# Sorted attention and a bilinear feed-forward: the output product by one level of Strassen's seven products

## The chip, the cores and the metric

The kernel runs on one core of a Trainium2 chip. Its engines work in parallel, each through its own queue in order: TensorE (PE in the profile; PEld is its loading of weights, which overlaps the matmuls), VectorE (DVE), ScalarE (ACT), GpSimd (POOL) and SyncE (SP), which here only issues DMAs. GpSimd issues the loads, SyncE the stores and the DMA transposes. The metric is the device time of one execution in microseconds (us); less is better.

## What is computed

```python
# q, k, v: (4, 8, 768, 64) = batch, heads, tokens, head size; sort_net: (4, 8, 8, 8)
P = sort_net
for _ in range(5):                                   # Sinkhorn
    P = np.exp(P - np.max(P, axis=-1, keepdims=True))
    P = P / (np.sum(P, axis=-1, keepdims=True) + 1e-09)
    P = P / (np.sum(P, axis=-2, keepdims=True) + 1e-09)
# blocks of 96 tokens; k and v become mixtures of their 8 blocks
k_sorted = np.einsum('bhij,bhjcd->bhicd', P, k_b)
v_sorted = np.einsum('bhij,bhjcd->bhicd', P, v_b)
scores = scale * np.matmul(q_b, k_sb.transpose(0, 1, 2, 4, 3))   # inside each block
attn = softmax(scores)
x = np.matmul(attn, v_sb)                            # heads side by side: (3072, 512)
out = ((x @ w_a) * (x @ w_b)) @ w_out                # 512 -> 1536 -> 512, float32
```

## The kernel before

Everything is computed in bf16 with f32 accumulation. Work goes by batch (4) and, in the attention, by pair of heads (4 pairs a batch, `g` counts all 16).

*Attention of one pair.* `stage_mix` (L265) multiplies k, and then v, by the expanded sort matrix `s_all` (24 matmuls for the two) and evicts the result into `kT` and `vT`; a DMA transpose turns `vT` into `vs` (L283). `stage_q` (L260) is the DMA transpose of q, from a copy that GpSimd makes (`pair_q`, L254). `stage_scores` (L286) multiplies and takes the exponential into `eT`. `stage_o` (L301) multiplies `eT` by `vs` (L241, with a column of ones for the sums), DVE takes the reciprocal (L245) and multiplies (L247), and `to_xT` (L307) transposes the result by DMA into `xT`.

*Batch 0* is done in two halves of four blocks each, with transposes on PE instead of by DMA: `half_q` (L170), `half_mix`, `half_scores`, `half_v`, `half_o`, `half_x`. Its q is loaded in two halves of 64 rows (`load_q_half`, L81), the second after the first weights. The four `half_q` of the first half run before the Sinkhorn chain has ended, the four of the second between the matmuls of the feed-forward.

*Feed-forward.* `ffn_ab(b, m, t)` (L331) makes one of the 12 row tiles `m` of the hidden layer for half `t` of the batch's 768 tokens: four matmuls of 384 columns with `w_a`, four with `w_b` (L323), ACT casts the first result (L343), DVE multiplies (L344) into `hT`. `ffn_out(b, c)` (L347) makes 128 output rows: 12 matmuls of 512 columns (L351) accumulate in one bank, ACT or DVE copies it (L160, L162), SyncE stores it.

*Order.* PE, GpSimd and SyncE run in the order in which the program is written; DVE and ACT are ordered by a scheduler, but for the head of the kernel. `interleave` (L529) spreads the pieces of the next batch's attention ("units") over the steps of the feed-forward of this batch: 12 `ffn_ab` and 6 `ffn_out` in the second half of batch 0, 24 and 6 in a later batch. Units come as mix, output of the pair before, scores. The loads of pair `g + 4` are issued with the mix of pair `g`; GpSimd is not tied to PE's progress but by the buffers it needs, of which `ld` has 8 for each of k, v and q.

*PSUM.* `psA` has two buffers of two banks (mix, scores, output), `psF` four of one bank (feed-forward and the small transposes).

*Head.* Five Sinkhorn rounds alternate ACT and DVE; PE then waits with warm-up matmuls (`keep_busy`, L164) for the replicated matrix and brings it into columns (`to_columns`, L410), from which `s_all` is spread.

Of the kernel before, what the change touches and what calls it, by code (L numbers as in the profile page):

```python
# [22 lines left out]
def kernel(  # L23
# [11 lines left out]
    nc = tc.nc  # L35
# [11 lines left out]
    HP = H // 2  # L47
    KA = DMODEL // P
    KO = DFF // P
    NBH = NB // 2  # L50
# [6 lines left out]
    HW = S // 2  # L57
    PSUM = bass.MemoryType.PSUM
# [3 lines left out]
    ld = ctx.enter_context(tc.tile_pool(name="ld", bufs=8))  # L62
    qtp = ctx.enter_context(tc.tile_pool(name="qtp", bufs=5))
    xtp = ctx.enter_context(tc.tile_pool(name="xtp", bufs=2))
    att = ctx.enter_context(tc.tile_pool(name="att", bufs=4))
    ffp = ctx.enter_context(tc.tile_pool(name="ffp", bufs=2))
    psA = ctx.enter_context(tc.tile_pool(name="psA", bufs=2, space=PSUM))
    psF = ctx.enter_context(tc.tile_pool(name="psF", bufs=4, space=PSUM))

# [9 lines left out]
    q_first = const.tile([P, H, W], BF16, name="q_first")  # L79

    def load_q_half(h):  # L81
        nc.gpsimd.dma_start(out=q_first[h * PH:(h + 1) * PH],
                            in_=_ap(q, h * PH * W, [[W, PH], [S * D, H], [1, W]]))

    loaded = {}

    def load_pair(b, hp):
        tiles = []
        for name, t in (("k2", k), ("v2", v), ("q2", q)):
            base = (b * H + 2 * hp) * S * D  # L90
            if b == 0 and name == "q2":
                continue
            to = ld.tile([P, 2, W], BF16, tag=name, name=name)
            nc.gpsimd.dma_start(out=to, in_=_ap(t, base, [[W, P], [S * D, 2], [1, W]]))  # L94
            tiles.append(to)
        loaded[b * HP + hp] = tiles

# [3 lines left out]
    WC = 256  # L101
# [12 lines left out]
    load_q_half(0)  # L114
    make_identity(nc, ident, nomemset=True)
    for hp in range(HP):
        load_pair(0, hp)
    load_ab(0)
    load_q_half(1)
    load_ab(1)  # L120
# [3 lines left out]
    NBUF = 3  # L124
# [45 lines left out]
    def half_q(h, hp, eng):  # L170
        q_ps = psF.tile([P, NCH, PH], BF16, tag="F", name="q_ps")
        rows = slice(h * PH, (h + 1) * PH)
        for c in range(NCH):
            for e in range(2):
                nc.tensor.matmul(q_ps[e * D:(e + 1) * D, c, :],  # L175
                                 lhsT=q_first[rows, 2 * hp + e, c * D:(c + 1) * D],
                                 rhs=ident[rows, rows], is_transpose=True)
        qT = qtp.tile([P, NB, NCH, CG], BF16, tag="qT", name="qT")
        copy(eng, qT[:, 0:NBH].rearrange("p i c t -> p c i t"),
             q_ps.rearrange("p c (i t) -> p c i t", i=NBH))  # L180
        st["q", h, hp] = qT
# [18 lines left out]
    def half_scores(h, hp):  # L200
        g = h * HP + hp
        kT, qT, eT = kTs[g % NBUF], st["q", h, hp], eTs[g % NBUF]
        sc = psA.tile([P, 2, 512], FP32, tag="A", name="sc")
        for i in range(NBH):
            for e in range(2):
                nc.tensor.matmul(  # L206
                    sc[:, e, i * BLK:(i + 1) * BLK],
                    lhsT=kT[e * D:(e + 1) * D, i * BLK:i * BLK + P],
                    rhs=qT[e * D:(e + 1) * D, i], start=True, stop=True)
# [43 lines left out]

    def pair_q(g):  # L254
        qc = qtp.tile([P, NCH, 2, D], BF16, tag="qc", name="qc", bufs=3)
# [4 lines left out]
    def stage_q(g):  # L260
# [4 lines left out]
    def stage_mix(g, what, engines):  # L265
# [10 lines left out]
        for hf, eng in enumerate(engines):  # L276
            n = 2 // len(engines)
            for u in range(n):
                d1 = _ap(to, (hf + u) * 3 * CG, [[whole, P], [CG, 3], [pitch, NB], [1, CG]])
                s1 = _ap(mix, (hf + u) * 512, [[1024, P], [P, 3], [CG, NB], [1, CG]])  # L280
                copy(eng, d1, s1)
        if what == "v":
            nc.sync.dma_start_transpose(out=vss[g % NBUF][:, :, V0:V0 + P],  # L283
                                        in_=to.rearrange("p i t -> p (i t)"))

    def stage_scores(g):  # L286
# [14 lines left out]
    def stage_o(g):  # L301
        xp = att.tile([BLK, NB, 2, D], BF16, tag="xp", name="xp")
        for hf in range(2):
            one_o(eTs[g % NBUF], hf, vss[g % NBUF], hf * NBH, xp, NB)
        st[g, "xp"] = xp

    def to_xT(g):  # L307
        xT, xp = xT_of(g // HP), st[g, "xp"]
        nc.sync.dma_start_transpose(
            out=xT[:, g % HP, :].rearrange("p (i t) -> p i t", i=NB),  # L310
            in_=xp.rearrange("p i e d -> p (i e d)"))
# [19 lines left out]
    def ffn_ab(b, m, t, begun=()):  # L331
        hT = hT_of(b)
        ab = []
        for n, w_sb in enumerate((w_a_sb, w_b_sb)):
# [6 lines left out]
            if n == 0:  # L341
# [3 lines left out]
                             in1=ab[1][:, 0:HW])  # L345

    def ffn_out(b, c):  # L347
        hT = hTs[b]
        po = psF.tile([P, DMODEL], FP32, tag="F", name="po")
        for m in range(KO):  # L350
            nc.tensor.matmul(po, lhsT=hT[:, m, c * P:(c + 1) * P], rhs=w_out_sb[:, m, :],  # L351
                             start=(m == 0), stop=(m == KO - 1))
        o_sb = ffp.tile([P, DMODEL], FP32, tag="o_sb", name="o_sb", bufs=3)
        copy("act" if c % 2 == 0 else "dve", o_sb, po)
        if b == 0:
            h, u = divmod(c, 3)
            for c2 in range(2):
# [3 lines left out]
                    in_=o_sb[c2 * PH:(c2 + 1) * PH])  # L361
        else:
            rows = out[b * S:(b + 1) * S, :].rearrange("(p c) n -> c p n", c=NCH)
            nc.sync.dma_start(out=rows[c], in_=o_sb)


    with tc.manual_schedule(engines={ET.PE, ET.Pool, ET.SP}):
        with tc.manual_schedule(engines={ET.Activation, ET.DVE}):
# [3 lines left out]
            p_rep = const.tile([BH, NB * NB, CG // 2], FP32, name="p_rep")  # L372
            for it in range(5):
# [20 lines left out]
                if it == 3:  # L394
                    half_q(0, 0, "act")
                    half_q(0, 1, "act")
            half_q(0, 2, "act")
            half_q(0, 3, "act")
# [4 lines left out]
            NR = NBH * NB  # L403

            def replicate(eng, hf):
                eng.tensor_copy(
                    out=p_rep[:, hf * NR:(hf + 1) * NR],
                    in_=_ap(p_fin, hf * NR, [[NB * NB, BH], [1, NR], [0, CG // 2]]))
# [9 lines left out]
            replicate(nc.vector, 0)  # L418
            replicate(nc.gpsimd, 1)
# [41 lines left out]

        for c in range(4, 6):
            load_ab(c)
        for hp in range(2):
            load_pair(1, hp)
        spread(nc.gpsimd, p_col, 8, 8)
        for c in range(3):
            load_out(c)
        pair_q(HP)
        pair_q(HP + 1)  # L470
        for hp in range(2, HP):
            load_pair(1, hp)
        for g in range(2, 4):
            spread(nc.gpsimd, p_col, g * 8, 8)


        def units_half():
            Q = [lambda hp=hp: half_q(1, hp, "dve") for hp in range(HP)]

            def M(hp):  # L480
                half_mix(1, hp, "k", "act")
                half_mix(1, hp, "v", "act")

            def R(hp):
                half_scores(1, hp)
                half_v(1, hp)

            us = [Q[0], lambda: M(0), Q[1]]
            for hp in range(HP):
                if hp + 1 < HP:  # L490
                    us.append(lambda hp=hp: M(hp + 1))
                us.append(lambda hp=hp: R(hp))
                if hp + 2 < HP:
                    us.append(Q[hp + 2])
                if hp > 0:
                    us.append(lambda hp=hp: half_x(1, hp - 1, "dve"))
                us.append(lambda hp=hp: half_o(1, hp))
            us.append(lambda: half_x(1, HP - 1, "dve"))
            return us

        def units_full(b):
            g0, us = b * HP, []

            def c_(g):
                if g == HP:
                    stage_q(g)
                if g + 1 < B * HP:
                    stage_q(g + 1)
                if g + 2 < B * HP:
                    pair_q(g + 2)  # L510
                if g + HP < B * HP:
                    load_pair((g + HP) // HP, g % HP)
                stage_mix(g, "k", ("act",))
                stage_mix(g, "v", ("dve", "act"))

            def o_(g):
                stage_o(g)
                to_xT(g)

            for n in range(HP + 1):  # L520
                if n < HP:
                    us.append(lambda g=g0 + n: c_(g))
                if n > 0:
                    us.append(lambda g=g0 + n - 1: o_(g))
                if n < HP:
                    us.append(lambda g=g0 + n: stage_scores(g))
            return us

        def interleave(steps, units, spare, slow=0):  # L529
            n, done = len(steps), 0  # L530
            for s, step in enumerate(steps):
                step()
                want = s + 1 if s < slow else -(-(s + 1) * len(units) // (n - spare))
                while done < min(want, len(units)):
                    units[done]()
                    done += 1
# [6 lines left out]
        steps = [lambda m=m: ffn_ab(0, m, 1) for m in range(KO)]  # L543
        steps += [lambda c=c: ffn_out(0, c) for c in range(NCH)]
# [37 lines left out]
```

## Time and profile before

| | us |
|---|---|
| time, median of 3 runs | 259.95 |
| the three runs | 255.99, 259.95, 264.06 |
| profiled execution: its span (its own time is not given beside it) | 252.7 |
| PE matmuls of `ffn_ab` (L323), in all | 155.6 |
| PE matmuls of `ffn_out` (L351), in all | 64.5 |
| DVE multiplies of `ffn_ab` (L344), in all | 52.6 |
| the stretch from the last matmul's end to the end of the span | 3.95 |

The profile's page gives busy time by engine, the span in 40 slices of 6.3 us, the chain of waits that ended last, and groups of instructions with their mean duration. Matmuls overlap, so the mean duration of one (326 ns for 384 columns) is not the distance between two; the distance is read from a run of them in the chain. The granted clock of PE was 0.993 over the span. Loads and transposes share the DMA engines: up to about 90 us these are busy throughout, afterwards for a third of the time.

### The profile page before, as it was taken

The numbers are of one execution on the slowest core, as the hardware profiler recorded it, in microseconds if no ns is written. First come the engines' busy times: TensorE is split into PE (matmuls) and PEld (weight loads), VectorE is DVE, ScalarE is ACT, GpSimd is POOL, SyncE is SP. The second block draws the span as 40 slices with busy tenths as digits, with TensorE's granted clock in tenths as the row PEclk, the third lists the DMA queues.
The fourth block names the chain that finished last, engine by engine and source line by source line (L and its number), as shares of the span: only waits on it lengthen the run. The fifth ranks groups of instructions, "written<-read, shape, count | busy, mean of one in ns | idle before, by whom it ended". The sixth has DMA issues, their size and how long they took to land.

```text
span 252.7 us, 5448 instructions
## 1 busy us (share of the span) xinstructions
PE 234.4 (93%) x2219; PEld 135.6 (54%) x2229; DVE 108.2 (43%) x259; ACT 102.4 (41%) x202; POOL 61.4 (24%) x83
## 2 busy tenths in 40 slices
PE   0999899969958999999999999999999999999993
PEld 0475566536624455666654456666654466665441
DVE  6775456535613313555453133645533144444111
ACT  3385555556520217463740137465440033333010
POOL 8974678554715305300100000000000000000000
PEclk9999999999997999999999999999999999999999
DMA  6999999999999998992332343332244210000122
GB/s 88 197 199 196 197 200 201 190 169 184 146 129 199 239 204 160 160 116 45 72 65 83 115 118 73 67 74 40 42 35 125 113 44 0 0 0 4 52 114 83
DMA packets 56441, 28.67 MB, mean 113 GB/s; under 512 B 33376, under 2 KB 53344, under 8 KB 56416
## 3 DMA queue, kind: packets, MB, share of 16 engines
q0 software_dynamic: 20944, 14.16, 40.6%
q1 hardware_dynamic: 35472, 14.17, 28.9%
q8 instruction: 17, 0.28, 0.4%
q14 instruction: 8, 0.07, 0.1%
HBM read 28.32 MB, written 6.29 MB: 137 GB/s over the span
## 4 chain that ended last, share of the span: by engine, by line
PE 83%; DMA 9%; DVE 5%; ACT 1%; issue 1%; DVEq 0%
PE pf L323 46%; PE po L351 24%; DMA vs<-vT 8%; PE o_ps L241 3%; PE mix L272 3%; PE sc L293 2%; PE mixh L191 2%; PE vs_ps L218 1%; PE sc L206 1%; PE xt_ps L232 1%; DMA p_nat<-in_sort_net_dram 1%; DVE hT L344 1%; DVE xph L247 1%; DVE csum L384 1%; ACT p_nat L374 1%
## 5 line engine op out<-in xcount | busy, mean ns | idle before, releaser
L344 DVE TENSOR_TENSOR hT<-a_sb,pf 128x384 bf16<-128x384 bf16 x95 | 52.6, 554 | 74.0 <-PE pf L323 45.5
L323 PE MATMUL pf<-xT,w_a_sb 128*128 128x384 bf16 x380 | 78.1, 327 | 0.0
L323 PE MATMUL pf<-xT,w_b_sb 128*128 128x384 bf16 x380 | 77.5, 326 | 0.0
L343 ACT CAST a_sb<-pf 128x384 bf16<-128x384 f32 x95 | 45.5, 479 | 65.9 <-PE pf L323 49.4
L351 PE MATMUL po<-w_out_sb,hT 128*128 128x512 bf16 x279 | 64.5, 385 | 0.5
L323 PEld LDWEIGHTS <-w_b_sb 128*128 128x128 bf16 x384 | 37.5, 98 | 25.1 <-issue 0.6
L323 PEld LDWEIGHTS <-w_a_sb 128*128 128x128 bf16 x384 | 34.6, 98 | 22.1
L351 PEld LDWEIGHTS <-hT 128*128 128x128 bf16 x288 | 28.0, 99 | 33.3 <-issue 1.6
L162 DVE COPY o_sb<-po 128x512 f32<-128x512 f32 x12 | 8.3, 692 | 47.8 <-PE po L351 31.3
L160 ACT COPY o_sb<-po 128x512 f32<-128x512 f32 x12 | 7.0, 586 | 43.0 <-PE po L351 23.1
L298 ACT ACTIVATE eT<-sc 96x768 bf16<-96x768 f32 x24 | 18.1, 802 | 12.4 <-PE sc L293 12.4
L256 POOL COPY qc<-q 128x768 bf16<-128x768 bf16 x12 | 9.9, 826 | 53.1 <-DMA qTf<-qc 34.0
L241 PE MATMUL o_ps<-vs,eT 96*128 96x65 bf16 x256 | 11.6, 196 | 6.1 <-DMA vs<-vT 5.4
L247 DVE TENSOR_TENSOR xp<-o_ps,rec 96x512 bf16<-96x512 f32 x24 | 15.5, 680 | 0.3
L241 PEld LDWEIGHTS <-eT 96*128 96x128 bf16 x256 | 10.5, 99 | 8.9 <-issue 6.3
L160 ACT CAST kT<-mix 128x384 bf16<-128x384 f32 x24 | 10.3, 482 | 6.2 <-PE mix L272 6.2
L94 POOL DMA_DIRECT2D v<-in_v_dram x16 | 11.5, 718 | 1.8 <-DMA w_b_sb<-in_moe_w_b_dram 0.8
L94 POOL DMA_DIRECT2D k<-in_k_dram x16 | 11.5, 719 | 1.2 <-DMA w_a_sb<-in_moe_w_a_dram 0.6
L245 DVE RECIPROCAL rec<-o_ps 96x8 f32<-96x8 f32 x32 | 5.2, 185 | 12.1 <-PE o_ps L241 12.0
L94 POOL DMA_DIRECT2D q<-in_q_dram x12 | 8.6, 719 | 1.3 <-DMA w_a_sb<-in_moe_w_a_dram 0.7
L175 PE MATMUL q_ps<-ident,q_first 64*64 64x64 bf16 x96 | 3.0, 217 | 6.2 <-DMA q_first<-in_q_dram 6.2
L210 ACT ACTIVATE eT<-sc 96x768 bf16<-96x768 f32 x8 | 6.5, 808 | 2.5 <-PE sc L206 2.5
(69 smaller groups left out, 138.4 us busy)
## 6 DMA issues: line engine op xcount, KB each, us to landing
out_dram<-o_sb SPq DMA_DIRECT2D x18, 256.0 KB, 2.0
k<-in_k_dram POOLq DMA_DIRECT2D x16, 192.0 KB, 6.4
v<-in_v_dram POOLq DMA_DIRECT2D x16, 192.0 KB, 6.8
q<-in_q_dram POOLq DMA_DIRECT2D x12, 192.0 KB, 9.1
w_a_sb<-in_moe_w_a_dram POOLq DMA_DIRECT2D x6, 256.0 KB, 10.8
w_b_sb<-in_moe_w_b_dram POOLq DMA_DIRECT2D x6, 256.0 KB, 10.7
w_out_sb<-in_moe_w_out_dram POOLq DMA_DIRECT2D x3, 512.0 KB, 10.9
out_dram<-o_sb SPq DMA_DIRECT2D x12, 128.0 KB, 5.1
```

The costliest lines, as they stand in the source:

```text
L94: nc.gpsimd.dma_start(out=to, in_=_ap(t, base, [[W, P], [S * D, 2], [1, W]]))
L160: nc.scalar.copy(out=out, in_=in_)
L162: nc.vector.tensor_copy(out=out, in_=in_)
L241: nc.tensor.matmul(o_ps[:, e, i * (D + 1):(i + 1) * (D + 1)], lhsT=eT[:, hf, e, i * BLK:i * BLK + P], rhs=vs[0:BLK, i0 + i, V0 - 1 + e * ( ...
L247: nc.vector.tensor_tensor(out=_ap(xp, i0 * 2 * D, [[nxp * 2 * D, BLK], [D, 2], [2 * D, NBH], [1, D]]), in0=_ap(o_ps, 1, [[1024, BLK], [511 ...
L256: nc.gpsimd.tensor_copy(out=qc.rearrange("p c e d -> p e c d"), in_=loaded[g][2].rearrange("p e (c d) -> p e c d", c=NCH))
L272: nc.tensor.matmul(mix[e * D:(e + 1) * D, c // 3, c % 3 * P:(c % 3 + 1) * P], lhsT=src2[:, e, c * D:(c + 1) * D], rhs=s_all[:, 2 * g + e], ...
L298: nc.scalar.activation(out=eT[:, hf, :, 0:HB], in_=sc[0:BLK, :, 0:HB], func=AF.Exp, scale=float(scale))
L323: nc.tensor.matmul(pf[:, 0:HW], lhsT=w_sb[:, kc, m * P:(m + 1) * P], rhs=x_cols(b, kc, t), start=(kc == 0), stop=(kc == KA - 1))
L343: nc.scalar.copy(out=a_sb, in_=pf[:, 0:HW])
L344: nc.vector.tensor_mul(out=hT[:, m, t * HW:(t + 1) * HW], in0=a_sb, in1=ab[1][:, 0:HW])
L351: nc.tensor.matmul(po, lhsT=hT[:, m, c * P:(c + 1) * P], rhs=w_out_sb[:, m, :], start=(m == 0), stop=(m == KO - 1))
```

## The change

The output product of two row chunks that lie 384 tokens apart (`u` and `u + 3`) is made together. With the hidden layer cut into 2 x 2 blocks A (tokens by hidden rows) and `w_out` into 2 x 2 blocks B (hidden rows by output columns), seven products of half the depth and half the width replace eight:

A22(B21-B11), (A11+A12)B22, A11(B12-B22), (A21+A22)B11, (A11+A22)(B11+B22), (A12-A22)(B21+B22), (A21-A11)(B11+B12).

GpSimd makes the five sums of B once (`weight_sums`), DVE the five sums of A for each hidden tile, as soon as its two tiles are there (`h_sums`, so `ffn_ab` takes the tiles in the order 0, 6, 1, 7, ...; two of the sums overwrite `hT`). ACT evicts three PSUM banks of products, DVE combines them. All batches are done so, but for the last pair of row chunks of the last batch: there one chunk is made as before and the other in two column ranges (`ffn_out_cut`: 384, evicted by DVE and stored by SyncE; 128, evicted by ACT and stored by ACT's queue).

With it: q of batch 0 is loaded by heads instead of by rows, its second half behind pair 0, and all of it is transposed on PE before the Sinkhorn chain ends (`first_q`), evicted by ACT (`first_q_out`); ACT instead of GpSimd makes one of the two replicas. A batch's units stand in the order M0 M1 R0 M2 R1 O0 M3 R2 O1 R3 O2 O3 (mix, scores, output). `pair_q` and the q transpose of pair `g + 1` follow the mix and the value transpose of pair `g`; loads of pair `g + 4` are issued at the output of pair `g`; `ld` has 6 buffers, `qc` 2, and the feed-forward's tiles one each.

```diff
-    ld = ctx.enter_context(tc.tile_pool(name="ld", bufs=8))
+    ld = ctx.enter_context(tc.tile_pool(name="ld", bufs=6))
-    ffp = ctx.enter_context(tc.tile_pool(name="ffp", bufs=2))
+    ffp = ctx.enter_context(tc.tile_pool(name="ffp", bufs=1))
+    outp = ctx.enter_context(tc.tile_pool(name="outp", bufs=1))
...
-    load_q_half(0)
+    load_q_first(0, HP)
     make_identity(nc, ident, nomemset=True)
-    for hp in range(HP):
-        load_pair(0, hp)
-    load_ab(0)
-    load_q_half(1)
-    load_ab(1)
+    load_pair(0)
+    load_q_first(HP, HP)
+    for g in range(1, HP):
+        load_pair(g)
+    for c in range(2):
+        load_ab(c)
...
+    def first_q(hp):
+        q_ps = psF.tile([P, NCH, P], BF16, tag="F", name="q_ps")
+        for c in range(NCH):
+            for e in range(2):
+                nc.tensor.matmul(q_ps[e * D:(e + 1) * D, c, :],
+                                 lhsT=q_first[:, 2 * hp + e, c * D:(c + 1) * D],
+                                 rhs=ident, is_transpose=True)
+        st["q_ps", hp] = q_ps
...
-    def stage_o(g):
+    def pair_o(g):
         xp = att.tile([BLK, NB, 2, D], BF16, tag="xp", name="xp")
+        if g + HP < NPAIR:
+            load_pair(g + HP)
...
+        if t == 1 and m >= KH:
+            h_sums(b, m - KH)
...
+    def weight_sums():
+        for n, (x, y, op) in enumerate(((B11, B22, ALU.add), (B12, B22, ALU.subtract),
+                                        (B21, B11, ALU.subtract), (B11, B12, ALU.add),
+                                        (B21, B22, ALU.add))):
+            t = const.tile([P, KH, NH], BF16, name=f"w_sum{n}")
+            nc.gpsimd.tensor_tensor(out=t, in0=x, in1=y, op=op)
+            w_sums.append(t)
...
+    def h_sums(b, m):
+        n = HW - P if b == B - 1 else HW
...
+        a11, a12, a21, a22 = (h_part(b, r, c, m)[:, 0:n] for r in range(2) for c in range(2))
+        s1, s2, s3 = (t[:, m, 0:n] for t in sums[b])
+        for to, x, y, op in ((s1, a11, a22, ALU.add), (s2, a21, a22, ALU.add),
+                             (s3, a11, a12, ALU.add), (a21, a21, a11, ALU.subtract),
+                             (a12, a12, a22, ALU.subtract)):
+            nc.vector.tensor_tensor(out=to, in0=x, in1=y, op=op)
+
+    def product(to, lhs, rhs, u):
+        for m in range(KH):
+            nc.tensor.matmul(to, lhsT=lhs(m)[:, u * P:(u + 1) * P], rhs=rhs[:, m],
+                             start=(m == 0), stop=(m == KH - 1))
...
+        def part1():
+            ps = psF.tile([P, 2, NH], FP32, tag="F", name="po45")
+            product(ps[:, 0], a22, w_sums[2], u)
+            product(ps[:, 1], hs[2], B22, u)
+            staged("s45", ps, 2)
...
+        def part3():
+            s45, s32, s1 = v["s45"], v["s32"], v["s1"]
+            ps = psF.tile([P, 2, NH], FP32, tag="F", name="po76")
+            product(ps[:, 0], a12, w_sums[4], u)
+            product(ps[:, 1], a21, w_sums[3], u)
...
+            for x, n in ((s45, 0), (s32, 1)):
+                nc.vector.tensor_tensor(out=rest[:, n], in0=x[:, 0], in1=x[:, 1],
+                                        op=ALU.subtract)
...
+            first_q_out(1, "act")
+            first_q_out(2, "act")
+            replicate("dve", 0)
+            replicate("act", 1)
+            first_q_out(3, "act")
...
+        halves = [n for m in range(KH) for n in (m, m + KH)]
+        steps = [lambda m=m: ffn_ab(0, m, 1) for m in halves]
+        steps[8:8] = [weight_sums]
+        steps += outs(0)
+        interleave(steps, units_full(1), 5)
```

## The prediction, made before the changed kernel ran

> **What bounds the kernel now.** I read the shares of busy time first, then the 40 slices, then the table of busy time by stage, and last the chain of waits where the slices show holes.
>
> ```profile
> span 252.7 us, 5448 instructions
> PE 234.4 (93%) x2219; PEld 135.6 (54%) x2229; DVE 108.2 (43%) x259; ACT 102.4 (41%) x202; POOL 61.4 (24%) x83
> PE   0999899969958999999999999999999999999993
> PEclk9999999999997999999999999999999999999999
> DMA  6999999999999998992332343332244210000122
> ```
>
> TensorE (PE) works in 93% of the span, so the change is worth what it takes off PE's own queue. Three kinds of PE time can still go: work, holes, and slow clock. The holes lie at the start, in slices 8, 11 and 12 (counted from 0; one is 6.3 us), and at the end; slice 12 also shows a lower granted clock. All are inside the first 15 slices, where the DMA row stands at 8 or 9, or at the very end. By stage (columns: stretch, length, then busy PE, PEld, DVE, ACT, POOL, clock, DMA share, GB/s):
>
> ```profile
> 20.75:44.60 23.85, 22.78 (x332) 14.64 (x330) 13.18 (x32) 12.44 (x25) 16.45 (x21) 1.00 1.35 199
> 44.60:70.40 25.80, 23.60 (x285) 14.56 (x284) 12.35 (x26) 15.16 (x31) 15.07 (x18) 1.00 1.39 168
> 70.40:92.60 22.20, 18.71 (x119) 8.95 (x121) 5.32 (x11) 3.48 (x6) 5.82 (x8) 0.92 1.32 194
> ...
> 147.30:201.90 54.60, 54.49 (x488) 31.45 (x489) 23.06 (x47) 23.91 (x47) 0.00 (x0) 1.00 0.34 74
> ```
>
> From 92.6 us on PE never waits; between 44.6 and 92.6 it idles 2.20 + 3.49 = 5.7 us and loses 22.2 x 0.08 = 1.8 us to the clock. The chain (start, us, what) names the wait:
>
> ```profile
> 49.34 7.60 DMA vs<-vT
> 57.08 0.65 PE o_ps L241 x16
> ...
> 63.40 12.91 DMA vs<-vT
> 76.44 1.04 PE o_ps L241 x16
> 77.48 3.83 PE po L351 x12
> ...
> 139.46 7.93 PE po L351 x36
> ...
> 201.91 31.20 PE pf L323 x192
> ```
>
> Twice the attention product `o_ps` waits for the DMA transpose of the sorted values (2.12 and 3.33 us idle before it, by PE's timeline). After the second, 16 matmuls take 1.04 us where the first took 0.65, and 12 `po` take 3.83 where 36 later take 7.93: the slow clock.
>
> **The seven products.** 192 matmuls of 384 columns in 31.20 us are 0.1625 us each, 0.423 ns a column; 36 of 512 columns at 0.2203. A pair of row chunks costs 24 x 512 columns now: 5.20 us by the column rate, 5.29 by the `po` row. After it is 7 x 6 = 42 matmuls of 256 columns: 42 x 0.1083 = 4.55 us if only columns count. A fixed cost per matmul is bounded by `o_ps`: 16 matmuls of 65 columns, each with its own 128-column weights, take 0.50 us, 0.031 each against 0.0275 by columns, so at most 4 ns: 42 x 0.112 = 4.70. The saving is 0.50 to 0.74 us a pair; I take 0.60. Three pairs in each of three batches and two in the last, 11: **-6.6 us** (-5.5 to -8.1).
>
> The weight loads nearly double for this product; the `o_ps` row says that pairs of load and matmul can follow at 0.031 us, so 0.108 covers them. The Trainium skill, "TensorE: Matmul & The Clock Gate", section "LDWEIGHTS", has a load take its columns over 1.2 GHz, which for 128 is 107 ns and speaks against halving the matmul, as nothing would be left to spare. By it the sum would be the same as long as loads overlap fully, and lose whatever does not.
>
> **What the products add elsewhere.** DVE: 30 adds of 128x384 bf16 a batch. No row shows such an add. `xT` copies of 128x384 bf16 from bf16 take 0.352 us, casts from f32 0.557; I take 0.35 and keep 0.55. 30 x 0.35 = 10.5 us (16.5). Then 2.9 us a pair to combine: three f32 operations on 512 at 0.69 (the `o_sb` copy) and two on 256 at about 0.42, less two copies. In a full batch DVE goes from 23.1 to about 40 us, beside 53 us of PE: covered, at 0 us. Without cover it would be the excess. ACT evicts 2 x 0.586 + 0.37 = 1.54 us a pair beside 4.6 us of PE: nothing.
>
> The second half of batch 0 is tighter: 12 steps of 1.3 us and some 5 us of attention on PE, against 12 x 0.55 + 10.5 + some 5 = 22 us of DVE. The order of units now puts mix 7 straight behind output 4. Both its buffers in `psA` are held until DVE has done reciprocal (0.185) and multiply (0.68), twice, with up to four adds (1.4) queued between: **+2 us** (0 to 3).
>
> GpSimd makes five weight sums of 128x1536. From `s_all`, 2.034 us for 1024 and 1.108 for 512: 1.81 ns an element, so 2.96 each, 14.8 in all. They queue behind the copy of `q` for pair 7. The loads up to pair 7 are 9.44 MB in bf16, at 197 GB/s from 4.2 us on until 52; with the transpose of pair 5 that the copy's buffer waits for, about 58 to 62. So the sums run from there to 73 to 77, the third (needed first) ready by 67 to 71. PE comes to its first product at about 71 and to the fourth and fifth sum at 75. Behind them GpSimd queues `q` of pair 8 and the loads of pairs 9 to 11; SyncE's transpose of that `q` stands ahead of `xT` 5, 6 and the first stores, which so go out at about 78, and `xT` 7 at 84 (four stores of about 1 us between), to land near 88, just when batch 1 begins. **+1.5 us** (0 to 12.7; the top is the rival below).
>
> **Early q.** Four groups of 12 `q_ps` leave the middle of the next half batch: 4 x 0.31, and with them four DVE copies and two PE gaps next to them (0.36 and 0.61): **-2.0 us** (-1.3 to -2.2). The head pays. All 48 transposes, now of 128 columns, stand on PE before the warm-up and before the columns of the sort matrix:
>
> ```profile
> 6.21 1.49 PE L175 MATMUL q_ps<-ident,q_first 64*64 64x64 bf16 x48 [6.21 <-DMA q_first<-in_q_dram]
> 7.63 0.61 PE L166 MATMUL heat<-warm 128*128 128x512 bf16 x1
> 8.46 2.77 PE L166 MATMUL heat<-warm 128*128 128x512 bf16 x6 [0.22 <-issue]
> 11.56 0.26 PE L412 MATMUL pc_ps<-ident,p_rep 32*128 32x32 bf16 x4 [0.33 <-DVE p_rep L406]
> ```
>
> The second half of q comes behind k and v of pair 0: 384 KB twice at 197 GB/s after 6.2 us is 10.2. Two groups of transposes (1.5 us at this rate) end at 11.7, eight warm-up matmuls (3.6 us) at 15.3, where 11.56 was the start: +3.7. Should the clock rise on the way, the eight take 8 x 0.22: +1.9. I take **+3.0 us** (0 to 4). k and v of pairs 1 to 3 land 2 us later than now, still ahead of this use.
>
> **Longer pipeline and gated loads.** Output 4 now comes after mix 6, some 12 us behind mix 4 where it was 9.7 with the wait; output 7 12.6 behind mix 7. With six buffers instead of eight, and loads asked for at the outputs, fewer loads run beside the transposes from 60 to 76. Both waits and the slow clock go, **-7.2 us** (0 to -7.5). Late next is DVE or the weight sums, counted above. SyncE now does a value transpose before the next q transpose, which shortens the one that was late.
>
> **Split last tile.** The columns stay; the copy behind the last matmul falls from 0.69 to 0.586 - 384 x 0.00084 = 0.27 us (ACT's rate from 384 and 512), the last store to a quarter: **-0.6 us** (0 to -1).
>
> ```profile
> 248.75 0.69 DVE L162 COPY o_sb<-po 128x512 f32<-128x512 f32 x1 [4.49 <-PE po L351]
> 249.47 0.33 SPq L364 DMA_DIRECT2D out_dram<-o_sb  x1
> ```
>
> **Sum:** -6.6 + 2.0 + 1.5 - 2.0 + 3.0 - 7.2 - 0.6 = -9.9 us, a span of 242.8. The page gives no time around the span: 252.7 lies 3.3 under the fastest run shown and 7.25 under the median. With the same surroundings as the median, 250.05; if the spread of the runs is the DMA wait that goes, 246.1. I take 249.
>
> **Rivals.**
> *GpSimd and DVE hinder each other* (slower). DVE's adds read two SBUF tiles while the weight sums run. In the trace every DVE operation beside a GpSimd sum had an operand in PSUM, so no row excludes it. If DVE stands still for the 14.8 us, PE goes on by two steps (2.6 us) and stops for 12.2 to 12.7: 250.05 - 1.5 + 12.7 = 261.3, above the median before; with adds of 0.55 us, some 6 us more, 267. It decides from about 11.5 us of standstill; half of it gives 255. The Trainium skill, "SBUF — State Buffer", section "Who interferes with whom", has just this: a DVE instruction with two SBUF inputs and a GpSimd instruction that reads SBUF lock each other out for whole instructions. No row here shows that.
> *The transposes stay late.* Their issue is in the same full queues; then -7.2 is lost: 257. Against it: more distance and fewer loads beside them.
> *A matmul of 256 columns doesn't cover its weight load.* Loads show 0.098 us; added to each matmul, 42 x 0.206 = 8.7 us, +3.5 a pair, 290. Against it stands `o_ps`.
> *Seven products that are not fewer on PE*: the program holds 42 matmuls of 256 columns a pair, so the columns do fall by an eighth.
>
> **How the numbers follow.** Forecast 0.55 (249); late transposes 0.15 (257); hindering 0.20, spread from 250 to 267; uncovered loads 0.03; the rest 0.07 without a picture. About 2% is what a measurement of this kernel can tell from no change, 254.75 to 265.1. Faster: 0.55 + 0.06 + 0.04 = 0.65; within: 0.15 + 0.07 = 0.22; slower 0.13. Low end: no new waits and a head at +1.9 with the smaller surroundings, 243. High end 257.5 takes in the late transposes and the milder half of the hindering.
>
> **What would show it.** 42 matmuls a pair in 4.6 us; `o_ps` with no wait for `vs`, the clock at 1.00 between 70 and 92; `pc_ps` at 13.5 to 15.3 instead of 11.56; batch 2 some 1.8 us shorter than 54.6. I am wrong if adds last 1 us or more beside the weight sums, if PE waits in front of the first product, or if the wait for `vs` is still there.

## The result and the profile after

The changed kernel takes 266.42 us (median of 4 runs, 266.12 to 268.96), the kernel before 260.6 in the same comparison: 1.042 times as long, 95% interval 1.035 to 1.049. Slower, where 249 us were forecast. Ratios and intervals, here and below, are of the runs in the faster of the two states in which a kernel is found; medians are of all its runs. The page's first rows and slices of the kernel after:

```profile
span 266.9 us, 5986 instructions
PE 231.6 (87%) x2391; PEld 157.3 (59%) x2391; DVE 182.8 (68%) x419; ACT 115.2 (43%) x226; POOL 76.8 (29%) x87
PE   0698895899501999999999999999999999999994
PEclk9999999599955799999999999999999999999999
DMA  6999999918804992769699133623121531000024
```

PE has less to do than before, but stands still for more than two slices (10 to 12) and finds a slow clock after it. DVE's busy time has grown by 75 us. The stages (stretch, length, busy PE, PEld, DVE, ACT, POOL, clock, DMA share, GB/s):

```profile
24.88:53.80 28.92, 23.73 (x286) 14.76 (x285) 18.37 (x32) 12.26 (x25) 18.40 (x20) 0.88 1.30 191
53.80:85.90 32.10, 16.16 (x192) 9.96 (x190) 27.29 (x35) 10.82 (x22) 22.56 (x15) 0.81 0.46 71
...
112.20:164.90 52.70, 52.70 (x543) 36.69 (x542) 38.95 (x90) 26.98 (x53) 11.89 (x16) 1.00 0.73 131
164.90:217.65 52.75, 52.75 (x544) 36.69 (x542) 38.20 (x90) 26.98 (x53) 0.83 (x1) 1.00 0.34 77
```

From batch 1 on the change does what it says: PE is busy throughout, and batch 2 takes 52.75 us instead of 54.60. Everything is lost before 91 us. PE's timeline there, with the idle time before a group in brackets:

```profile
48.02 0.50 PE L241 MATMUL xt_ps<-ident,xph 96*128 96x96 bf16 x4 [4.49 <-DVE xph L256]
...
69.74 0.65 PE L250 MATMUL o_ps<-vs,eT 96*128 96x65 bf16 x16
86.07 0.85 PE L282 MATMUL mix<-s_all,k 128*64 128x128 bf16 x12 [15.68 <-DVE rec L254]
```

Both holes wait for DVE. What DVE did then (start, us), and beside it GpSimd:

```profile
42.08 5.29 DVE L417 TENSOR_TENSOR hs<-hT 128x384 bf16<-128x384 bf16 x1
...
67.61 15.05 DVE L417 TENSOR_TENSOR hs<-hT 128x384 bf16<-128x384 bf16 x2
```

```profile
42.42 3.96 POOL L158 TENSOR_TENSOR s_all<-mask,p_col 128x1024 bf16<-128x1024 bf16 x2
46.33 0.81 POOL L266 COPY qc<-q 128x768 bf16<-128x768 bf16 x1
...
66.30 15.25 POOL L402 TENSOR_TENSOR w_sum<-w_out_sb 128x1536 bf16<-128x1536 bf16 x5
```

The 72 adds into `hs` (least, median and longest, in ns):

```profile
L417 DVE TENSOR_TENSOR hs<-hT x72: 285/352/14157, 40.0 to 249.8; 128x384 bf16<-128x384 bf16 x54, 128x256 bf16<-128x256 bf16 x18
```

One lasts 5.29 us, another 14.16; their median is 0.35. The first ends 0.2 us after the two spreads and the copy of `q` behind them, the second 0.2 us after the last of the five weight sums. After each hole PE's clock is low: four `pf` matmuls take about 1.27 us instead of 0.65 for the next 4 to 6 us, some 2.5 us lost each time.

### The profile page after: what moved, and what is told of

It is laid out like the page before. It is cut to its first block, busy times and chain, and to the rows that moved or that the text cites. A ratio compares the mean times of both kernels' runs of the same rounds, so it can differ in the third digit from the quotient of the medians.

```text
span 266.9 us, 5986 instructions
## 1 busy us (share of the span) xinstructions
PE 231.6 (87%) x2391; PEld 157.3 (59%) x2391; DVE 182.8 (68%) x419; ACT 115.2 (43%) x226; POOL 76.8 (29%) x87
## 3 DMA queue, kind: packets, MB, share of 16 engines
q0 software_dynamic: 20944, 14.16, 37.4%
## 4 chain that ended last, share of the span: by engine, by line
PE 76%; DVE 13%; DMA 3%; issue 3%; POOL 2%; ACT 2%; DVEq 0%; ACTq 0%
PE pf L331 43%; PE po L421 18%; DVE hs L417 7%; PE mix L282 3%; DMA v<-in_v_dram 3%; PE o_ps L250 2%; DVE hT L352 2%; PE sc L302 2%; PE mixh L200 2%; DVE xp L256 1%; POOL k L100 1%; PE po L374 1%; PE po L384 1%; DVE hT L417 1%; PE xt_ps L241 1%
## 5 line engine op out<-in xcount | busy, mean ns | idle before, releaser
L417 DVE TENSOR_TENSOR hs<-hT 128x384 bf16<-128x384 bf16 (+1 forms) x72 | 42.7, 620 | 1.5
L421 PE MATMUL po<-w_sum,hT 128*128 128x256 bf16 x264 | 33.4, 273 | 0.2 <-DVE hT L352 0.2
L432 ACT COPY s<-po 128x512 f32<-128x512 f32 (+1 forms) x33 | 17.0, 515 | 30.4 <-PE po L421 27.6
L421 PEld LDWEIGHTS <-hs 128*128 128x128 bf16 x198 | 19.4, 98 | 2.2
L282 PE MATMUL mix<-s_all,k 128*64 128x128 bf16 x144 | 6.6, 230 | 15.7 <-DVE rec L254 15.7
L421 PE MATMUL po<-w_out_sb,hs 128*128 128x256 bf16 x132 | 18.0, 273 | 0.0
L402 POOL TENSOR_TENSOR w_sum<-w_out_sb 128x1536 bf16<-128x1536 bf16 x5 | 15.2, 3080 | 0.0
L417 DVE TENSOR_TENSOR hT<-hT 128x384 bf16<-128x384 bf16 (+1 forms) x48 | 14.7, 347 | 0.0
L456 DVE TENSOR_TENSOR o<-s,s 128x512 f32<-128x512 f32 x11 | 7.9, 714 | 7.7 <-ACT s L432 7.7
L461 DVE TENSOR_TENSOR rest<-s 128x256 f32<-128x256 f32 x22 | 9.2, 420 | 4.5 <-ACT s L432 4.1
```

The costliest lines, as they stand in the source:

```text
L282: nc.tensor.matmul(mix[e * D:(e + 1) * D, c // 3, c % 3 * P:(c % 3 + 1) * P], lhsT=src2[:, e, c * D:(c + 1) * D], rhs=s_all[:, 2 * g + e], ...
L402: nc.gpsimd.tensor_tensor(out=t, in0=x, in1=y, op=op)
L417: nc.vector.tensor_tensor(out=to, in0=x, in1=y, op=op)
L421: nc.tensor.matmul(to, lhsT=lhs(m)[:, u * P:(u + 1) * P], rhs=rhs[:, m], start=(m == 0), stop=(m == KH - 1))
L432: nc.scalar.copy(out=t, in_=ps)
```

## The experiments

**Theory A**: a DVE operation with two SBUF inputs (the adds of `h_sums`) and a GpSimd operation that reads SBUF keep each other out, and PE runs dry behind DVE. **Theory B**: mix 7 stands straight behind output 4 and finds its PSUM buffers held, whoever makes the sums.

### e1: the weight sums on DVE

```diff
-            nc.gpsimd.tensor_tensor(out=t, in0=x, in1=y, op=op)
+            nc.vector.tensor_copy(out=t[:, 0, 0:1], in_=hTs[0][:, 9, HW:HW + 1])
+            nc.vector.tensor_tensor(out=t, in0=x, in1=y, op=op)
```

(The one-element copy, which the sum overwrites, keeps the scheduler from moving the sums ahead of tile 9.)

> The five weight sums are made by DVE instead of GpSimd, behind hidden tile 9; nothing else changes. Theory A (DVE adds with two SBUF inputs and GpSimd sums that read SBUF keep each other out): no add beside them lasts over 1 us, PE's hole of 15.7 us at 70 to 86 us shrinks to the 2 to 5 us that five sums of about 0.95 us cost on DVE, the slow clock after it (about 2.6 us) goes too, and the hole of 4.5 us at 43 to 48 us stays, since the spreads of the sort matrix are still on GpSimd; time about 250 to 256. Theory B (mix 7 stands straight behind output 4 and finds its PSUM buffers held, whoever makes the sums): a hole of over 10 us stays; time 262 to 270.

252.81 us, 0.980 of before (0.973 to 0.986): 13.6 us less than the change, by the medians of two comparisons. PE's two holes in e1, and its row of all 72 adds to `hs` (least, median and longest, in ns):

```profile
48.07 0.41 PE L250 MATMUL o_ps<-vs,eT 96*128 96x65 bf16 x8 [3.06 <-DVE vs L228]
...
69.64 0.53 PE L282 MATMUL mix<-s_all,k 128*64 128x128 bf16 x12 [2.74 <-DVE w_sum L402]
```

```profile
L418 DVE TENSOR_TENSOR hs<-hT x72: 285/352/4061, 40.0 to 233.8; 128x384 bf16<-128x384 bf16 x54, 128x256 bf16<-128x256 bf16 x18
```

The first hole stays, at 3.06 us, and so does one long add, now of 4.06 us, beside the spreads. The 15.7 us have become 2.74, and 0.31 at the second half of the mix. That is within the 2 to 5 us expected, but not for the reason expected: it is not the price of the five sums (0.95 us each), which DVE makes only after the mix has begun:

```profile
68.82 0.68 DVE L256 TENSOR_TENSOR xp<-o_ps,rec 96x512 bf16<-96x512 f32 x1
...
70.25 1.81 DVE L403 TENSOR_TENSOR w_sum<-w_out_sb 128x1536 bf16<-128x1536 bf16 x2
```

(The row of PE names a one-element copy into `w_sum`, which stands beside the multiply in DVE's queue.) Mix 7 waits for output 4's reciprocal and multiply behind four adds. So theory B has these 3 us, and A the rest: the order of the units is the same in e1 and in the change. The slow clock behind this hole was expected to go and did not: it is at 0.50 from 71 to 74 us.

### e2: the same sums on GpSimd, in 30 pieces

```diff
-            nc.gpsimd.tensor_tensor(out=t, in0=x, in1=y, op=op)
+            for m in range(KH):
+                nc.gpsimd.tensor_tensor(out=t[:, m], in0=x[:, m], in1=y[:, m], op=op)
```

> GpSimd makes the weight sums in 30 pieces of 128x256 instead of 5 of 128x1536. Theory A1 (the engines exclude each other for one instruction at a time, and DVE gets its turn between two GpSimd instructions): an add lasts at most about 1 us, the hole falls below 8 us, time 254 to 260. Theory A2 (GpSimd keeps DVE out for as long as it has instructions ready): one add lasts about 15 us again, the hole is 15 to 17 us, time 265 to 269. Theory B: as A2 in time, but with adds of 0.35 us.

270.19 us (one run), span 268.3. DVE, GpSimd and PE in e2:

```profile
65.45 18.70 DVE L418 TENSOR_TENSOR hs<-hT 128x384 bf16<-128x384 bf16 x2
```

```profile
64.14 18.76 POOL L403 TENSOR_TENSOR w_sum<-w_out_sb 128x256 bf16<-128x256 bf16 x30
```

```profile
87.56 0.85 PE L282 MATMUL mix<-s_all,k 128*64 128x128 bf16 x12 [19.51 <-DVE rec L254]
```

A2: an add waits out all the pieces, though each lasts only 0.66 us. DVE gets no turn between two pieces. Hole and time lie above the 15 to 17 and 265 to 269 us expected, as the pieces take 18.8 us in all and the five whole sums 15.3.

### e3: the old output product in batch 0 only

```diff
-        if t == 1 and m >= KH:
+        if b > 0 and t == 1 and m >= KH:
             h_sums(b, m - KH)
...
-        steps += outs(0)
-        interleave(steps, units_full(1), 5)
+        steps += [lambda c=c: ffn_out(0, c) for c in range(NCH)]
+        interleave(steps, units_full(1), 2)
```

> Batch 0's output product is made with 12 matmuls of 512 columns as before the change, so DVE makes no sums of the hidden layer in batch 0; the seven products start with batch 1; the weight sums stay on GpSimd, in their place. Theory A: both holes (4.5 and 15.7 us) and the slow clock behind them (2.8 and 2.6 us) go, batch 0's output costs PE 1.9 us more; time 266.4 - 25.6 + 1.9 = 243, up to 248 if the transposes of the values are late again. Theory B: the hole of 15.7 us stays, at 262 or more.

254.42 us, 0.985 of before (0.979 to 0.992). Both holes are gone, as A says, but 243 to 248 was not reached. PE now waits at the start of batch 1:

```profile
93.47 0.48 PE L331 MATMUL pf<-xT,w_a_sb 128*128 128x384 bf16 x1 [4.02 <-DMA xT<-xp]
96.67 0.48 PE L331 MATMUL pf<-xT,w_a_sb 128*128 128x384 bf16 x1 [2.73 <-DMA xT<-xp]
```

The queues of SyncE and GpSimd in e3, and a part of its chain of waits:

```profile
75.55 1.22 SPq L272 DMA_TRANSPOSE qTf<-qc  x1
76.82 1.44 SPq L316 DMA_TRANSPOSE xT<-xp  x1
```

```profile
59.47 15.29 POOL L402 TENSOR_TENSOR w_sum<-w_out_sb 128x1536 bf16<-128x1536 bf16 x5
74.71 0.81 POOL L266 COPY qc<-q 128x768 bf16<-128x768 bf16 x1
```

```profile
78.96 9.27 DMA out_dram<-o_sb
...
90.14 6.49 DMA xT<-xp
```

The weight sums on GpSimd may have a second price: the copy of `q` for pair 8 queues behind them, SyncE's transpose of that copy waits, and `xT` stands behind it. This is the queue that the prediction followed to "just when batch 1 begins"; in the changed kernel it would be hidden, since PE is late itself. But it is not all. By the chain, the last transpose into `xT` comes behind stores whose copy waits 9.27 us for an earlier store to land, and e8, which has the old product and no weight sums at all, waits in the same place:

```profile
92.11 0.32 PE L330 MATMUL pf<-xT,w_a_sb 128*128 128x384 bf16 x1 [2.46 <-DMA xT<-xp]
93.60 0.32 PE L330 MATMUL pf<-xT,w_a_sb 128*128 128x384 bf16 x1 [1.17 <-DMA xT<-xp]
```

So of the 6.75 us in e3 the weight sums have at most the 3.1 by which it waits longer; the rest comes with the old product in batch 0. (The kernel before has three output tiles for it, e3 and e8 have two; this was not tried apart.)

### e4: the kernel before, with the weight sums added on GpSimd

```diff
+        steps[8:8] = [weight_sums]
```

(The sums go into one tile that nothing reads.)

> The kernel before, with the five weight sums added on GpSimd in the second half of batch 0 (into one tile that nothing reads). Theory A: DVE there has no operation with two SBUF inputs, so it is not held, and the time is that of before but for GpSimd's own queue (loads and copies of q behind the sums come up to 15 us later): 256 to 266. A theory that GpSimd sums disturb DVE, PE or the DMA whatever DVE does gives DVE operations longer than 1 us there.

256.49 us (one run), no slower than before, whose seven runs beside it took 257.47 us or more. GpSimd and DVE of e4:

```profile
65.64 15.75 POOL L554 TENSOR_TENSOR w_sum<-w_out_sb 128x1536 bf16<-128x1536 bf16 x5
```

```profile
67.52 0.55 DVE L344 TENSOR_TENSOR hT<-a_sb,pf 128x384 bf16<-128x384 bf16 x1 [1.56 <-ACT a_sb L343]
...
69.28 0.56 DVE L162 CAST vT<-mix 128x384 bf16<-128x384 f32 x1 [0.17 <-PE mix L272]
```

The sums on GpSimd without the adds (e4) cost nothing, the adds without sums on GpSimd (e1) little, both together 16 us of standstill. A multiply with one input in PSUM keeps its 0.55 us beside the sums.

### e5 to e7: the head, the collisions, and both

e5 is e1 with q loaded first:

```diff
-    load_pair(0)
     load_q_first(HP, HP)
-    for g in range(1, HP):
+    for g in range(HP):
         load_pair(g)
...
-            keep_busy(heat[:, 0], 8)
+            keep_busy(heat[:, 0], 4)
```

> The kernel of e1 with both halves of batch 0's q loaded ahead of k and v of pair 0, and four warm-up matmuls instead of eight. Theory: the head is late (pc_ps at about 15.2 instead of 11.56 us) because PE, in order, waits 2.5 us for the second half of q and then does the whole warm-up; now pc_ps starts at 11.5 to 12.0 and the time falls by 3 to 3.7 us against e1, to about 249. Rival: what follows waits for the loads or the value transposes anyway, and less than 1 us of it is left at the end (252 to 253).

253.14 us, 0.988 of before (0.981 to 0.995): nothing against e1's 252.81 and 0.980. The head did move, and the gain went into the next hole. PE there:

```profile
48.04 0.50 PE L240 MATMUL xt_ps<-ident,xph 96*128 96x96 bf16 x4 [5.22 <-DVE xph L255]
```

`pc_ps` starts at 11.56 us, as before the change. But the spreads on GpSimd still run at 42.4, when the DMA queue lets them; DVE arrives earlier and waits longer (an add of 5.42 us instead of 4.06), and the clock falls behind the hole, as it did not in e1. The rival's number (252 to 253) nearly came, its reason did not: neither theory of e5 had this.

e6 is e1 with the spreads moved ahead and the weight sums taken apart:

```diff
         load_pair(5)
+        for n in range(2, 4):
+            spread(nc.gpsimd, p_col, n * 8, 8)
         for c in range(3):
             load_out(c)
...
         load_pair(7)
-        for n in range(2, 4):
-            spread(nc.gpsimd, p_col, n * 8, 8)
...
+        def ab_and_sum(m):
+            ffn_ab(0, m, 1)
+            if m < 5:
+                weight_sum(m)
```

(`weight_sum(n)` makes sum n on DVE, held back by hidden tile n; `interleave` spares 4 steps instead of 5, as the list is one shorter.)

> The kernel of e1 with the two last spreads of the sort matrix moved in front of the loads of w_out, so that they end before DVE's first add with two SBUF inputs, and with the five weight sums on DVE taken apart, one behind each of the hidden tiles 0 to 4. Theory A: no add over 1 us in the whole trace; PE's holes of 3.1 us near 45 us and of 2.7 + 0.3 us near 69 us go, and the slow clock if the first of them caused any; against e1 4 to 6 us less, 247 to 249. If a hole of 2 us or more stays at mix 7, it is the order of the units and DVE's load, not the exclusion.

251.18 us, 0.980 of before (0.974 to 0.986): 1.6 us below e1 by the medians and nothing by the ratios, where 4 to 6 us were expected. The holes of e1 are gone but for 1.47 and 0.61 us at mix 7, which by the expectation are the order of the units and DVE's load; in their place comes the wait of the kernel before, in one place:

```profile
85.23 0.65 PE L250 MATMUL o_ps<-vs,eT 96*128 96x65 bf16 x16 [2.44 <-DMA vs<-vT]
```

e7 has both edits.

> e5 and e6 together: 244 to 246 if the two gains add (their places in the kernel are apart); over 247 if PE, being earlier, meets the loads of batch 1 or w_out too soon.

248.13 us (245.8 to 251.85), 0.963 of before (0.951 to 0.976). It is 3.1 us below e6 and 5.0 below e5, all measured in one comparison, and 2 us above the expected stretch: q loaded first, worth nothing in e5, is worth its 3 us where nothing swallows it. In e7 no add is held any more:

```profile
L417 DVE TENSOR_TENSOR hs<-hT x72: 284/355/523, 36.5 to 229.3; 128x384 bf16<-128x384 bf16 x54, 128x256 bf16<-128x256 bf16 x18
```

So the change, with its sums kept apart from GpSimd and q loaded first, beats the kernel before, by 2.4 to 4.9% in this comparison; e9 and e10, which differ little from it, got 0.974 and 0.975 in another.

### e8: e7 with the old output product everywhere

```diff
-            steps = [part for u in us for part in ffn_out_pair(b, u)]
+            if b < B - 1:
+                return [lambda c=c: ffn_out(b, c) for c in range(NCH)]
```

(Cut: `h_sums` and the weight sums go with it; the last batch makes five chunks so, and its last tile stays split.)

> The kernel of e7 with the output product as before the change in all batches (12 matmuls of 512 columns; no sums of weights or hidden layer); the last tile stays split. It measures the seven products alone, on a kernel without the two disturbances. By PE's columns they are worth 11 x 0.6 = 6.6 us: e8 at e7 + 6 to 7. If DVE's extra 64 us of work costs PE time somewhere, the difference is smaller; if there is none, the seven products gave nothing.

253.93 us (250.69 to 255.56), 0.983 of before (0.970 to 0.995). e8 lies 5.8 us above e7 by the medians and about 5 by the ratios (0.963 and 0.983), with intervals that overlap a little. This is not the price of the seven products alone. e8's trace, of the longest of its four runs, waits 3.6 us for `xT` where e7 does not (the two rows under e3), and its head is 1.4 us later (`pc_ps` at 13.30 and 11.86 us). The products are read better from batch 2, where PE is busy throughout in both: 52.88 us in e7 and 54.52 in e8, 1.64 for three pairs; in the changed kernel and the kernel before it is 52.75 and 54.60.

### e9 and e10: the order of units, and when the sums come

e9 is e7 with the units in the old order, e10 is e7 with the weight sums one hidden tile later:

```diff
-        order = [("M", 0), ("M", 1), ("R", 0), ("M", 2), ("R", 1), ("O", 0), ("M", 3),
-                 ("R", 2), ("O", 1), ("R", 3), ("O", 2), ("O", 3)]
+        order = [("M", 0), ("R", 0), ("M", 1), ("O", 0), ("R", 1), ("M", 2), ("O", 1),
+                 ("R", 2), ("M", 3), ("O", 2), ("R", 3), ("O", 3)]
```

> The kernel of e7 with the units in the order of the kernel before (mix, scores, then the output of the pair before: M0 R0 M1 O0 R1 M2 O1 R2 M3 O2 R3 O3), the rest unchanged. If the longer pipeline is what removed the waits for the value transposes, the o_ps waits for vs come back, 3 to 7 us with the clock: 251 to 255. If the fewer loads beside the transposes removed them, or DVE now makes PE late enough anyway, it is e7 within 1.5 us.

248.65 us, 0.974 of before (0.963 to 0.986): e7 within the noise. PE waits for `vs` twice in e9, 0.16 us at 56.68 and here:

```profile
76.12 0.65 PE L249 MATMUL o_ps<-vs,eT 96*128 96x65 bf16 x16 [1.28 <-DMA vs<-vT]
```

1.4 us of waiting, where the kernel before had 5.4. So the longer pipeline removed at most a quarter of it, by this one trace. Whether the gated loads or the later PE removed the rest was not tried apart.

```diff
-            if m < 5:
-                weight_sum(m)
+            if 0 < m < 6:
+                weight_sum(m - 1)
```

> The kernel of e7 with the five weight sums behind hidden tiles 1 to 5 instead of 0 to 4: in e7 DVE waited 2.0 us for w_out to land, and PE 2.2 us at the mix behind it. That hole goes: 1 to 2 us less than e7. If it stays, the mix waits for ACT's or DVE's own queue.

248.38 us, 0.975 of before (0.962 to 0.987): no gain. The 2.2 us hole behind DVE's wait for `w_out` is gone, but scores now wait 1.83 us for a q transpose, and the clock is at half behind that. This stretch is held by several things of the same size.

## Why the prediction was wrong

**The step that failed is the weight sums**, "+1.5 us (0 to 12.7)". Their duration was right (3.08 us each, 2.96 forecast), and the rival named what happens: DVE standing still while GpSimd sums. The sum took the value without it and gave the rival 0.20; in both runs that have such adds beside such sums (the changed kernel and e2) it came. Its price was too low as well. PE did go on for two steps (to 70.4 us), but the hole lasted 15.7 us and not 12.7: after the standstill DVE still had 3.4 us of adds, multiplies and reciprocals queued before the buffer that mix 7 waits for. The slow clock behind it, some 2.5 us, was not counted. At 266.4 the rival's far end (267) is about right, but by luck: it holds 6 us of slower adds that did not come and 5 us too much around the span.

**A second collision was not seen.** The rival looked at the adds beside the weight sums alone. The scheduler puts those adds that need only tiles of the first half as early as 40 us, into the two spreads on GpSimd: a hole of 4.49 us and 2.5 us of clock.

**The buffers of mix 7**, "+2 us (0 to 3)", were right: 2.1 us in e6, and 3.1 in e1, where a copy of `q` holds an add for 0.6. In the changed kernel they are part of the 3.4 us above.

Together: 18 us at the sums where 1.5 and 2 (the buffers of mix 7) stood, 7 at the spreads, 0.8 at the head: 22.3 of the 24.1 us between the forecast span (242.8) and the measured (266.9). The other 1.8 were not traced.

**Early q**: `pc_ps` at 15.35 us, the first number worked out (15.3); 3.0 was taken, 3.8 came. PE's timeline:

```profile
10.39 1.49 PE L181 MATMUL q_ps<-ident,q_first 128*64 128x128 bf16 x24 [2.62 <-DMA q_first<-in_q_dram]
11.82 3.59 PE L172 MATMUL heat<-warm 128*128 128x512 bf16 x8
15.35 0.27 PE L569 MATMUL pc_ps<-ident,p_rep 32*128 32x32 bf16 x4
```

The gain behind it was right: from the first `pf` of the chain to mix 4, 26.6 us before, 31.5 after, less 7 us of hole and clock: 2.1 saved, 2.0 forecast.

**The seven products** were right: `po` in three pairs, by the chain of waits,

```profile
153.94 4.59 PE po L421 x42
...
159.02 5.90 PE po L421 x54
```

4.59 us for 42 matmuls (4.55 to 4.70 worked out). The weight loads are covered: where the Trainium skill ("TensorE: Matmul & The Clock Gate", "LDWEIGHTS") leaves next to nothing to spare (107 ns for a load of 128 columns), matmuls of 256 columns follow at 109 ns here, so nothing was lost. Adds of 0.35 us and DVE under PE's cover in batches 1 to 3: right.

**Late transposes**: no wait for `vs` in the changed kernel, as forecast. But PE stands still for 16 us in this stretch there, so it is no test. Without that hole the same order of units has no such wait in e1, e3, e5, e7, e8 and e10 and 2.44 us in e6: the term was about right, but not for the reason given first (e9).

**The split last tile**: 3.30 us behind the last matmul instead of 3.95, forecast -0.6. ACT's copy and its store:

```profile
263.66 0.27 ACT L166 COPY o_cut<-po 128x128 f32<-128x128 f32 x1 [2.08 <-PE po L374]
263.95 0.37 ACTq L379 DMA_DIRECT2D out_dram<-o_cut  x1
```

**The time around the span** is 1.8 to 2.1 us in the runs after, less than the 3.3 and 7.25 considered; by that, the profiled execution before the change took about 254.7 us, 5 under the median then shown.

## What to carry to other kernels

Before work is given to two engines at once, put their instruction lists side by side and look at what each reads: here two cheap operations, 0.35 us on DVE and 3 us on GpSimd, cost PE 16 us because they met. A row of the trace that doesn't show an operation is no evidence that it is harmless, and a rival that nothing in the trace excludes, and whose operations the program surely puts side by side, deserves more than a fifth. A gain in front of a fixed obstacle is worth nothing until the obstacle goes: e5 alone gave 0, with e6 it gave 3 us.

## What the runs showed of the hardware

A DVE add with two SBUF inputs (0.35 us by itself) that meets GpSimd instructions reading SBUF is held until a run of them ends, and was not let in between two of a kind that follow each other: neither between 5 sums of 3.08 us (14.16 us for one add in the changed kernel) nor between 30 of 0.66 us (18.7 us for two adds in e2) nor between two spreads (5.29 us). Between the last of such instructions and a copy of `q` behind them it was let in once: in the changed kernel the long add ended at 81.77 us, 0.2 after the last sum, and the copy held the next add (0.97 us); in e2 the add waited for the copy too. Why, no run shows. That the two keep each other out is what the Trainium skill says ("SBUF — State Buffer", section "Who interferes with whom"); it has this for one whole instruction, and the runs show it for a whole run of them.

A GpSimd copy with one input holds an add as well (0.89 us at 51.78 beside `qc` in the changed kernel), and DVE operations with an input in PSUM are not touched (0.55 us in e4). GpSimd's sums, which came first, were not slowed: 3.08 us with the adds waiting beside them and without. The copy of `q`, 0.83 us by itself, took 0.95 and 0.97 us where it began beside such an add (81.50 us in the changed kernel, 67.45 in e1).

How long PE must stand still for its clock to fall, these traces do not settle: behind 3.06 us in e1 it stayed at 1.00, behind 1.83 us in e10 it was 0.50 from 60 to 62 us, and behind the same two waits at mix 7 it fell in e7 (0.50 from 68 to 70 us) and not in e6.
